# Two weight loads moved from SyncE's queue to ScalarE's at the start of a fused S5 scan and GeGLU kernel

## The chip, the cores and the metric

The kernel runs on one core of one Trainium2 chip. The metric is the device time of one execution in microseconds (us). Before the change three runs took 179.05 to 179.17 us, with a median of 179.15 us.

The engines are called PE (TensorE, matrix products), ACT (ScalarE), DVE (VectorE), POOL (GpSimd) and SP (SyncE, which here only issues DMAs). ACT can issue DMAs too, on a queue of its own.

## The reference

The input is x of 2048 tokens by 512 features. It is normalised, goes through a complex diagonal recurrence (S5) and, beside it, through a gated feed-forward block of width 1376, and the two are multiplied and added to x:

```python
def _B_ref(x, w_gate, w_up, w_down):
    return (_gelu(x @ w_gate) * (x @ w_up)) @ w_down

# _A_ref: Bu = x @ B_bar^T (complex, 512 states); h_t = Lam_bar * h_(t-1) + Bu_t
#         y = 2 * Re(h @ C^T) + x * Dskip
x = A_x
xn = _layernorm(x, axis=-1)
s = _A_ref(xn, A_Lambda_re, A_Lambda_im, A_B_re, A_B_im, A_C_re, A_C_im, A_log_dt, A_Dskip)
g = _silu(_B_ref(xn, B_w_gate, B_w_up, B_w_down))
return x + s * g
```

All arrays are in bfloat16. The weights `w_gate` and `w_up` are 512 by 1376 (1.4 MB each), `w_down` is 1376 by 512.

## The kernel before

**Stages.** The tokens are cut into four slabs of 512 (`NS = 4`), each of four tiles of 128 tokens (`M = 4`). The 512 features are four k slices of 128 (`KT = 4`). The 1376 columns of the gate and up weights are three pieces (`CH`): 0 to 512, 512 to 1024 and 1024 to 1376, the last one with 352 columns.

For every slab the kernel normalises x, turns it (a transposing DMA into `xnT`), multiplies it with the up and gate weights (`gate_tile`, one group of four matmuls for each piece), multiplies gate and up, turns the product (`at_t`), multiplies with `w_down` (`down_pair`), and beside this runs the recurrence (`half`: products with `BT`, then rotations and scans on DVE) and the output product with C (`y_tile`).

**The first slab is special.** Its up and gate products do not wait for the whole normalisation. For tile 0, ACT sums columns 320 to 512 (L411, the first activation that reads x) and DVE columns 0 to 320 (L414), DVE subtracts both partial means (L418, two halves), PE turns the centred tile with four small matmuls (`head_t`, L387; L400 for the tiles 1 to 3), and DVE and ACT copy the result into `W` (L391, L393, L402). For the tiles 1 to 3 ACT makes the whole mean (L423) and DVE subtracts it (L424). Then single matmuls (`up_rows`, L462, one for a tile, a k slice and a piece of 512 columns) and groups of four (`first_w`, L499, for the 352-column piece and for the gate weights) use the centred tile; the factor 1/std is put in when ACT takes the result out of PSUM (L471, L505). Seven dummy matmuls on a constant (L375) run on PE from the start.

**Loads.** The weights come in pieces, so that PE can begin early: `load_w("wu", k0, k1, c0, c1, end, landed)` loads the k slices k0 to k1 and the columns c0 to c1. The first up piece is k slice 0, columns 0 to 512 (128 KB); the 352-column up piece is all four k slices of the columns 1024 to 1376 (352 KB). All x and weight loads are issued by SP; ACT issues three loads of 1 KB each, the parameters of the recurrence (L333), before L411.

**Order.** Each operation is a step of a list (`Plan.add`). `ORDER` is a fixed list of step numbers that a planner wrote beforehand from a cost for each step (for a load: `end` and `landed` are the due times of its issue and its landing, in us) and that `Plan.run` follows: it gives the order of the instructions on every engine's queue. `SLOTS` fixes the buffer of each group: six PSUM banks for groups of 512 columns ("ps") and two for part groups ("pp"). A bank is used again when the engine that reads its result is through.

**Completion semaphores.** In the built program the DMAs of both queues take eight completion semaphores in turn, in the order in which the steps are emitted. A DMA that takes a semaphore for a second time has a wait in front of it, in the queue of the engine that issues it, until the DMA that held it before has landed. Before the change the first eight are the x tiles 0, 1 and 2 (SP), parameter 0 (ACT), an up piece (SP), parameter 1 (ACT), an up piece (SP) and parameter 2 (ACT); the DMAs from the ninth on are all SP's.

Of the kernel before, what the change touches and what calls it, by code (L numbers as in the profile page):

```python
# [17 lines left out]
PE, ACT, DVE, POOL, SP = "PE", "ACT", "DVE", "POOL", "SP"  # L18


ORDER = (
# [24 lines left out]
)  # L46
SLOTS = {
# [4 lines left out]
    ),  # L52
    "pp": (
        0, 1, 0, 1, 0, 1, 0, 1, 0, 0, 0, 1, 0, 1, 0, 1, 0, 1, 0, 1, 1, 0, 1, 0, 1, 1, 1, 0, 0, 0, 0, 1, 1, 0, 1, 0, 1, 0, 1,
    ),
    "U": (
        0, 1, 0, 2, 0, 1, 0, 2,
    ),
    "g2": (
        5, 0, 1, 4, 3, 0, 4, 2, 2, 0, 1, 5, 3, 1, 4, 5,  # L60
    ),
    "at": (
        2, 0, 1, 3, 2, 1, 0, 0, 0, 1, 2, 3, 2, 3, 0, 1,
    ),
    "gtA": (
        0, 0, 1, 1, 0, 1, 0, 1, 1, 0, 0, 0, 1, 1, 0, 0,
    ),
    "gtB": (
        1, 1, 0, 0, 0, 0, 1, 1, 1, 0, 0, 0, 0, 1, 0, 1,
    ),  # L70
    "ubA": (
        0, 1, 0, 0, 1, 1, 1, 0, 0, 0, 1, 1,
    ),
    "ubB": (
        0, 0, 1, 1, 1, 0, 0, 1, 0, 0, 1, 0,
    ),
    "yg": (
        0, 0, 1, 1, 0, 1, 0, 1, 0, 1, 1, 0, 0, 0, 1, 0, 1, 0,
    ),
    "ot": (  # L80
        1, 1, 1, 0, 1, 0, 0, 0, 0, 0, 0, 1, 1, 0, 1, 0, 1,
    ),
    "sk": (
        2, 3, 0, 1, 5, 7, 4, 6, 0, 1, 3, 2, 5, 4, 6, 7,
    ),
    "atT": (
        0, 1, 3, 0, 1, 1, 3, 2, 0, 3, 2, 1, 1, 2, 3, 0,
    ),
}

# [58 lines left out]
def kernel(  # L149
# [17 lines left out]
    nc = tc.nc  # L167
# [3 lines left out]
    F = 1376  # L171
    KT = D // P
# [9 lines left out]
    CH = [(0, 512), (512, 1024), (1024, F)]  # L182
# [6 lines left out]
    V, A, G, T = nc.vector, nc.scalar, nc.gpsimd, nc.tensor  # L189
# [6 lines left out]
    def sb(name, shape, dt=BF16):  # L196
        return consts.tile(shape, dt, name=name)
# [4 lines left out]
    wu = sb("wu", [P, KT, F])  # L202
# [10 lines left out]
    W2 = CH[1][1]  # L213
# [51 lines left out]
    def dma(eng, issue, land, emit, reads=(), writes=(), **kw):  # L265
        return pl.add(eng, issue, emit, reads, writes, lag=land, **kw)
# [11 lines left out]
    def dma_sp(end, landed, emit, writes, **kw):  # L278

        n = dma(SP, end - sp_at[0], landed - end, emit, writes=writes, after=list(sp_last), not_before=sp_at[0], svc=(1, 0.0, 0.0), **kw)  # L280
        sp_at[0] = end
        sp_last[:] = [n]

    def load_w(nm, k0, k1, c0, c1, end, landed):

        w, r = w_of[nm]
        dma_sp(end, landed, lambda: nc.sync.dma_start(out=w[:, k0:k1, c0:c1], in_=r[:, k0:k1, c0:c1]),  # L287
               [(nm, k, c) for k in range(k0, k1) for c in range(3) if c0 <= CH[c][0] < c1])

    def load_slab(s, **kw):  # L290
        dma(SP, 0.8, 4.0, lambda: nc.sync.dma_start(out=x_tok[:, s * M : (s + 1) * M, :], in_=x_r[:, s * M : (s + 1) * M, :]),
# [3 lines left out]
    def load_x(m, end, landed):  # L295
        dma_sp(end, landed, lambda: nc.sync.dma_start(out=x_tok[:, m, :], in_=x_r[:, m, :]), [("x", 0, m)])  # L296

    W1 = CH[0][1]
    load_x(0, 1.12, 2.92)
    load_x(1, 1.59, 3.35)  # L300
    load_x(2, 2.06, 3.75)
    load_w("wu", 0, 1, 0, W1, 2.53, 4.4)
    load_w("wu", 0, 1, W1, W2, 3.0, 4.95)
    load_w("wu", 1, 2, 0, W1, 3.47, 5.5)
    load_w("wu", 1, 2, W1, W2, 3.94, 6.05)
    load_x(3, 4.41, 6.6)
    load_w("wu", 2, 3, 0, W1, 4.88, 7.15)
    load_w("wu", 2, 3, W1, W2, 5.35, 7.7)
    load_w("wu", 3, 4, 0, W2, 5.82, 8.8)
    load_w("wu", 0, KT, W2, F, 6.29, 10.0)  # L310
    load_w("wg", 0, KT, W1, F, 6.76, 12.4)
    load_w("wg", 0, KT, 0, W1, 7.23, 14.0)
    for ri, src in enumerate((A_B_re, A_B_im)):
# [18 lines left out]
    for i, (t, v) in enumerate(((pv0[0:4, :], A_log_dt), (pv1[0:4, :], A_Lambda_im), (pv1[4:8, :], A_Lambda_re))):  # L332
        first = [dma(ACT, 0.48, 1.7, lambda t=t, v=v: A.dma_start(out=t, in_=v.rearrange("(k p) -> k p", p=P)),  # L333
                     writes=[("pv", i)], rank=900.0, not_before=0.8, after=first)]
# [440 lines left out]
    c1, s1 = cbt[:, :, 1], sbt[:, :, 1]  # L775
# [32 lines left out]
    for pt in range(NPT):  # L808
# [3 lines left out]
            out=C2[:, 0, pt, :], in0=CT[:, 0, pt, :], scalar=cre[:, pt : pt + 1], in1=tF[:, 1, :], op0=ALU.mult, op1=ALU.subtract),  # L812
            ["coef", ("CT", 0), ("tF",)], [("C2", 0, pt)], base=0.13)
        dve(512, lambda pt=pt: V.scalar_tensor_tensor(
            out=C2[:, 1, pt, :], in0=CT[:, 1, pt, :], scalar=ncre[:, pt : pt + 1], in1=tF[:, 0, :], op0=ALU.mult, op1=ALU.subtract),
# [104 lines left out]
```

## Time and profile before

| | |
|---|---|
| median of three runs | 179.15 us (179.05 to 179.17) |
| profiled execution, first to last instruction (span) | 176.9 us |
| PE busy | 172.1 us, 97% of the span |
| DVE busy | 154.6 us, 87% |
| ACT busy | 132.6 us, 75% |
| DMA queue used by SP | 18.52 MB, 46.7% of the 16 DMA engines' span |

The median is the time of the whole execution; the span leaves out what lies before the first and after the last instruction, 2.25 us here. Busy shares are averages over the span: an engine can be the limit in one stage and idle in another. Lines such as L411 are those of the kernel before; after the change the same lines stand three or four lines lower (L411 becomes L414, L462 becomes L465).

### The profile page before, as it was taken

How to read it: one execution, taken by the hardware profiler on the slowest of the kernel's cores; microseconds unless marked ns; L12 is line 12 of the kernel's file. 1: busy time of each engine (PE TensorE's matmuls, PEld its weight loads, DVE VectorE, ACT ScalarE, POOL GpSimd, SP SyncE). 2: the span in 40 equal slices, each digit the busy share in tenths (PEclk: the TensorE clock that was granted, in tenths of full speed). 3: DMA queues.
4: the chain of work that ended last, by engine and by line, in shares of the span. 5: the costliest groups of instructions: out<-in, count | busy, mean ns of one | idle time of the engine just before them, and what ended most of it. 6: DMA issues, size and time to landing. Idle time of an engine off the chain costs nothing.

```text
span 176.9 us, 2418 instructions
## 1 busy us (share of the span) xinstructions
PE 172.1 (97%) x834; PEld 82.3 (47%) x849; DVE 154.6 (87%) x253; ACT 132.6 (75%) x246; POOL 10.9 (6%) x25
## 2 busy tenths in 40 slices
PE   8999999999999999999999999999999999999992
PEld 2554544454454444444444444444444444444451
DVE  3743799999999988999999699999999999999343
ACT  6679999989999999956697665735898860793310
POOL 2640500000200000011000000000000000000000
PEclk9999999999999999999999999999999999999999
DMA  5999999997092730040057050063007300550531
GB/s 150 285 347 247 160 288 189 305 217 158 8 193 43 138 62 4 0 82 0 0 115 150 2 111 0 0 126 70 0 11 154 87 0 4 129 123 0 113 119 30
DMA packets 48467, 18.66 MB, mean 105 GB/s; under 512 B 40296, under 2 KB 48328, under 8 KB 48456
## 3 DMA queue, kind: packets, MB, share of 16 engines
q1 hardware_dynamic: 48432, 18.52, 46.7%
q8 instruction: 6, 0.10, 0.2%
q14 instruction: 5, 0.04, 0.1%
q10 hardware_dynamic: 24, 0.00, 0.0%
HBM read 6.46 MB, written 2.10 MB: 48 GB/s over the span
## 4 chain that ended last, share of the span: by engine, by line
PE 94%; DMA 2%; SPq 1%; issue 1%; DVE 0%
PE bank L536 31%; PE bank L564 21%; PE bank L615 16%; PE bank L579 16%; PE bank L499 7%; PE bank L462 3%; DMA wu<-in_B_w_up_dram 2%; SPq L296 1%; SPq L287 0%; DVE yg L585 0%; DVE ot L586 0%; PE bank L400 0%
## 5 line engine op out<-in xcount | busy, mean ns | idle before, releaser
L536 PEld LDWEIGHTS <-xnT 128*128 128x128 bf16 x288 | 28.1, 98 | 29.4
L564 PE MATMUL bank<-wd,atT 128*128 128x512 bf16 (+1 forms) x174 | 40.2, 379 | 0.1
L536 PE MATMUL bank<-wu,xnT 128*128 128x512 bf16 (+1 forms) x140 | 31.9, 356 | 0.1
L536 PE MATMUL bank<-wg,xnT 128*128 128x512 bf16 (+1 forms) x139 | 31.7, 356 | 0.3
L615 PE MATMUL bank<-xnT,BT 128*128 128x512 bf16 x128 | 30.9, 379 | 0.1
L646 DVE TENSOR_TENSOR_SCAN Fs<-rho,ini,W 128x512 bf16<-128x512 f32 x24 | 29.8, 1272 | 0.1
L579 PE MATMUL bank<-C,hst 128*128 128x512 bf16 (+1 forms) x134 | 29.7, 366 | 0.1
L564 PEld LDWEIGHTS <-atT 128*128 128x128 bf16 (+1 forms) x176 | 17.2, 98 | 20.3
L539 ACT ACTIVATE ubA<-bank 128x512 bf16<-128x512 f32 x24 | 14.6, 614 | 8.8 <-PE bank L536 8.3
L617 ACT ACTIVATE U<-bank 128x512 bf16<-128x512 f32 x32 | 19.1, 622 | 1.7 <-PE bank L615 1.7
L579 PEld LDWEIGHTS <-hst 128*128 128x128 bf16 x136 | 13.3, 98 | 14.0
L615 PEld LDWEIGHTS <-BT 128*128 128x128 bf16 x128 | 12.5, 98 | 14.3
L627 DVE TENSOR_TENSOR Q<-U,tab 128x4096 bf16<-128x4096 bf16 x8 | 18.3, 2287 | 0.7 <-ACT tab L715 0.6
L539 ACT ACTIVATE gtA<-bank 128x512 bf16<-128x512 f32 x24 | 14.8, 616 | 5.3 <-PE bank L536 4.6
L627 DVE TENSOR_TENSOR Q<-Fs,tab 128x4096 bf16<-128x4096 bf16 x8 | 18.3, 2285 | 0.1
L567 ACT ACTIVATE g<-bank 128x512 f32<-128x512 f32 x16 | 9.2, 594 | 12.1 <-PE bank L564 12.1
L585 DVE TENSOR_TENSOR yg<-bank,g 128x512 bf16<-128x512 f32 (+1 forms) x17 | 11.1, 655 | 5.0 <-PE bank L579 4.6
L539 ACT ACTIVATE ubB<-bank 128x352 bf16<-128x352 f32 x12 | 5.7, 475 | 6.6 <-PE bank L536 5.5
L838 ACT ACTIVATE junk<-x_tok 128x512 bf16<-128x512 bf16 x16 | 10.2, 649 | 0.0
L499 PE MATMUL bank<-wg,W 128*128 128x512 bf16 (+1 forms) x47 | 9.7, 356 | 0.1
L843 ACT ACTIVATE xna<-x_tok,nb,rs 128x512 bf16<-128x512 bf16 x12 | 9.6, 876 | 0.0
L575 ACT ACTIVATE bank<-sk 128x512 f32<-128x512 bf16 (+1 forms) x17 | 9.5, 577 | 0.1
(121 smaller groups left out, 190.0 us busy)
## 6 DMA issues: line engine op xcount, KB each, us to landing
out_dram<-ot SPq DMA_DIRECT2D x15, 128.0 KB, 1.8
x_tok<-in_A_x_dram SPq DMA_DIRECT2D x3, 512.0 KB, 5.6
wd<-in_B_w_down_dram SPq DMA_DIRECT2D x1, 1280.0 KB, 7.1
wg<-in_B_w_gate_dram SPq DMA_DIRECT2D x1, 864.0 KB
wu<-in_B_w_up_dram SPq DMA_DIRECT2D x6, 128.0 KB, 3.3
x_tok<-in_A_x_dram SPq DMA_DIRECT2D x4, 128.0 KB, 2.2
wg<-in_B_w_gate_dram SPq DMA_DIRECT2D x1, 512.0 KB, 7.8
wu<-in_B_w_up_dram SPq DMA_DIRECT2D x1, 352.0 KB, 3.9
```

The costliest lines, as they stand in the source:

```text
L499: T.matmul(ps[:, 0 : b - a], lhsT=xcT[:, k, m * P : (m + 1) * P], rhs=wt[:, k, a:b], start=(k == 0), stop=(k == KT - 1))
L536: T.matmul(ps[:, 0 : b - a], lhsT=xnT[:, s % 2, m, k, :], rhs=wt[:, k, a:b], start=(k == 0), stop=(k == KT - 1))
L539: acts(b - a, lambda: act(out=dst, in_=ps[:, 0 : b - a], func=AF.Copy if up else AF.Gelu_apprx_tanh), [key], [ok], table=None if up else " ...
L564: T.matmul(ps[:], lhsT=atT[:fs, k, iT * P : (iT + 1) * P], rhs=wd[:fs, k, :], start=(k == 0), stop=(k == NFT - 1))
L579: T.matmul(ps, lhsT=hst[s % 2][:, j // NPT, j % NPT, m * P : (m + 1) * P], rhs=C2[:, j // NPT, j % NPT, c0:c1], start=False, stop=(j == 2 ...
L585: dve(w, lambda: V.tensor_tensor(out=yg[iy][:, 0:w], in0=ps, in1=g2[ig][:, c0:c1], op=ALU.mult), [key, ("g2", gg)], [("yg", gy)])
L615: T.matmul(ps[:], lhsT=BT[:, ri, k, pt * P : (pt + 1) * P], rhs=xnT[:, s % 2, :, k, :], start=(k == 0), stop=(k == KT - 1))
L617: acts(512, lambda q=q, ri=ri, ps=ps: act(out=U[ui][:, ri, q, :], in_=ps[:], func=AF.Copy), [key], [("U", ug, q, ri)])
L627: dve(4096, lambda: V.tensor_tensor(out=Qf, in0=src.unsqueeze(1).to_broadcast(WQ), in1=table, op=ALU.mult), reads, ["Q"], rate=2.0)
L646: pl.add(DVE, 1.12 if s == 0 else 1.185, lambda ri=ri, q=q, pt=pt, first=first: V.tensor_tensor_scan(out=Fs[:, ri, q, :], data0=rho[:, pt ...
L838: acts(512, lambda i=i, fn=fn, sc=sc, m=m: act(out=junk()[:], in_=x_tok[:, s * M + m, :], func=fn, scale=sc, accum_out=sx[:, s, i, m : m + ...
L843: acts(512, lambda m=m: act(out=xn[m], in_=x_tok[:, s * M + m, :], func=AF.Identity, scale=rs[:, s, m : m + 1], bias=nb[:, s, m : m + 1]), ...
```

## The change

`load_w` gets a flag that puts a load on ACT's queue. Two loads use it: the first up piece, and the 352-column up piece. The other loads stay on SP, in the order of the listing without those two.

```diff
-    def load_w(nm, k0, k1, c0, c1, end, landed):
+    def load_w(nm, k0, k1, c0, c1, end, landed, act_queue=False):
         w, r = w_of[nm]
-        dma_sp(end, landed, lambda: nc.sync.dma_start(out=w[:, k0:k1, c0:c1], in_=r[:, k0:k1, c0:c1]),
-               [(nm, k, c) for k in range(k0, k1) for c in range(3) if c0 <= CH[c][0] < c1])
+        keys = [(nm, k, c) for k in range(k0, k1) for c in range(3) if c0 <= CH[c][0] < c1]
+        if act_queue:
+            dma(ACT, 0.43, landed - end, lambda: A.dma_start(out=w[:, k0:k1, c0:c1], in_=r[:, k0:k1, c0:c1]), writes=keys)
+            return
+        dma_sp(end, landed, lambda: nc.sync.dma_start(out=w[:, k0:k1, c0:c1], in_=r[:, k0:k1, c0:c1]), keys)
...
-    load_w("wu", 0, 1, 0, W1, 2.53, 4.4)
+    load_w("wu", 0, 1, 0, W1, 2.53, 4.4, act_queue=True)
...
-    load_w("wu", 0, KT, W2, F, 6.29, 10.0)
+    load_w("wu", 0, KT, W2, F, 6.29, 10.0, act_queue=True)
```

`ORDER` and `SLOTS` are written anew by the planner: the same 692 steps in another order and in other buffers, on every engine. On ACT the two loads follow the three parameter loads and stand ahead of the first activation on x. On PE the matmuls of the first slab change places: after the first tile's transposes come single up matmuls of the k slices 0 and 1, eight of them in a row before the first group on the 352-column piece, which before came after six. On SP the last x slab is loaded after the first transposing load of C and no longer before the transpose of slab 1, and the large part of `w_down` follows two transposes of `at` later.

More of the change, by code (lines that the diff above doesn't have):

```diff
@@ L48 @@
     "ps": (
[3 rows of a table removed]
[3 rows of a table added]
     ),
     "pp": (
-        0, 1, 0, 1, 0, 1, 0, 1, 0, 0, 0, 1, 0, 1, 0, 1, 0, 1, 0, 1, 1, 0, 1, 0, 1, 1, 1, 0, 0, 0, 0, 1, 1, 0, 1, 0, 1, 0, 1,
+        0, 0, 1, 0, 0, 1, 0, 1, 1, 1, 1, 0, 1, 1, 0, 0, 0, 0, 1, 1, 1, 1, 0, 0, 1, 0, 1, 0, 0, 1, 1, 0, 0, 0, 1, 1, 1, 0, 1,
     ),
     "U": (
-        0, 1, 0, 2, 0, 1, 0, 2,
+        1, 0, 2, 1, 0, 2, 0, 1,
     ),
     "g2": (
-        5, 0, 1, 4, 3, 0, 4, 2, 2, 0, 1, 5, 3, 1, 4, 5,
+        2, 1, 0, 5, 4, 2, 5, 3, 0, 5, 1, 3, 2, 1, 4, 0,
     ),
     "at": (
-        2, 0, 1, 3, 2, 1, 0, 0, 0, 1, 2, 3, 2, 3, 0, 1,
+        2, 1, 0, 3, 2, 0, 1, 0, 0, 2, 3, 1, 2, 0, 3, 1,
     ),
     "gtA": (
-        0, 0, 1, 1, 0, 1, 0, 1, 1, 0, 0, 0, 1, 1, 0, 0,
+        1, 1, 0, 1, 1, 1, 0, 0, 0, 1, 0, 1, 0, 1, 1, 0,
     ),
     "gtB": (
-        1, 1, 0, 0, 0, 0, 1, 1, 1, 0, 0, 0, 0, 1, 0, 1,
+        0, 0, 0, 1, 0, 1, 0, 0, 1, 1, 0, 1, 0, 0, 1, 1,
     ),
     "ubA": (
-        0, 1, 0, 0, 1, 1, 1, 0, 0, 0, 1, 1,
+        0, 0, 1, 1, 0, 1, 0, 1, 1, 0, 0, 1,
     ),
     "ubB": (
-        0, 0, 1, 1, 1, 0, 0, 1, 0, 0, 1, 0,
+        1, 1, 0, 1, 0, 1, 1, 0, 0, 1, 1, 0,
     ),
     "yg": (
-        0, 0, 1, 1, 0, 1, 0, 1, 0, 1, 1, 0, 0, 0, 1, 0, 1, 0,
+        0, 0, 1, 1, 1, 0, 1, 1, 1, 1, 0, 0, 0, 1, 0, 0, 1, 0,
     ),
     "ot": (
-        1, 1, 1, 0, 1, 0, 0, 0, 0, 0, 0, 1, 1, 0, 1, 0, 1,
+        1, 1, 1, 0, 0, 1, 1, 1, 0, 0, 0, 1, 1, 0, 1, 0, 1,
     ),
     "sk": (
-        2, 3, 0, 1, 5, 7, 4, 6, 0, 1, 3, 2, 5, 4, 6, 7,
+        2, 0, 1, 3, 5, 4, 6, 7, 2, 0, 3, 1, 7, 6, 4, 5,
     ),
     "atT": (
-        0, 1, 3, 0, 1, 1, 3, 2, 0, 3, 2, 1, 1, 2, 3, 0,
+        1, 3, 0, 0, 1, 2, 3, 2, 2, 0, 1, 3, 1, 2, 0, 0,
     ),
```

54 rows, old and new, of tables (ORDER, SLOTS) are left out of this document.

## Prediction

> **What bounds the kernel now.** I read the page first, then the chain that ended last in order of time, then the timeline of the first 24 us engine by engine. The page says who is busy, and what the chain of waits is made of:
>
> ```profile
> span 176.9 us, 2418 instructions
> PE 172.1 (97%) x834; PEld 82.3 (47%) x849; DVE 154.6 (87%) x253; ACT 132.6 (75%) x246; POOL 10.9 (6%) x25
> PE 94%; DMA 2%; SPq 1%; issue 1%; DVE 0%
> ```
>
> The chain in order of time shows where the other 6% lie (columns: start us, us, what):
>
> ```profile
> 1.18 0.41 SPq L296
> ...
> 2.58 0.43 SPq L287
> ...
> 3.06 3.89 DMA wu<-in_B_w_up_dram
> ...
> 6.99 1.35 PE bank L499 x8
> ...
> 8.78 0.60 PE bank L499 x4
> 9.38 0.86 PE bank L462 x4
> ...
> 172.01 1.76 PE bank L579 x16
> ```
>
> From 6.99 us, when the 352-column up piece has landed (issued at 3.06), to 173.77 us TensorE is the chain without a break. So the end is 6.99 us plus 166.8 us of matmuls that follow back to back, and only two things can move it: how much of TensorE's work is done by 7 us, and whether the new order leaves TensorE waiting later. An up matmul of 512 columns takes 0.86 / 4 = 0.215 us of the chain, a 352-column group of four 0.60 us. The span is 176.9 us, the median run 179.15 us; the 2.25 us between them I leave as they are, and every term below is added to the median.
>
> The first 7 us on ACT, on DVE and on TensorE (columns: start us, us, instruction):
>
> ```profile
> 1.66 0.32 ACTq L333 DMA_DIRECT2D pv<-in_A_Lambda_re_dram  x1
> ...
> 2.88 0.36 ACT L411 ACTIVATE junk<-x_tok 128x192 bf16<-128x192 bf16 x1 [0.67 <-DMA x_tok<-in_A_x_dram]
> 3.15 0.19 ACT L411 ACTIVATION_READ_ACCUMULATOR junk<-x_tok 128x1 f32 x1
> 3.44 0.63 ACT L423 ACTIVATE junk<-x_tok 128x512 bf16<-128x512 bf16 x1
> 3.97 0.19 ACT L423 ACTIVATION_READ_ACCUMULATOR junk<-x_tok 128x1 f32 x1
> 4.06 0.61 ACT L423 ACTIVATE junk<-x_tok 128x512 bf16<-128x512 bf16 x1
> ```
>
> ```profile
> 3.49 0.60 DVE L418 TENSOR_SCALAR xna<-x_tok,ma,mb 128x256 bf16<-128x256 bf16 x2
> 4.19 0.35 DVE L424 TENSOR_SCALAR xna<-x_tok,ma 128x512 bf16<-128x512 bf16 x1
> 4.46 0.28 DVE L391 COPY W<-bank 128x256 bf16<-128x256 bf16 x1
> 4.80 0.35 DVE L424 TENSOR_SCALAR xna<-x_tok,ma 128x512 bf16<-128x512 bf16 x1
> ```
>
> ```profile
> 3.90 0.66 PE L387 MATMUL bank<-ident,xna 128*128 128x128 bf16 x4
> 4.60 0.40 PE L400 MATMUL bank<-ident,xna 128*128 128x128 bf16 x4
> 4.84 0.38 PE L462 MATMUL bank<-wu,W 128*128 128x512 bf16 x1
> 5.21 0.40 PE L400 MATMUL bank<-ident,xna 128*128 128x128 bf16 x4
> ...
> 5.67 1.25 PE L462 MATMUL bank<-wu,W 128*128 128x512 bf16 x5
> ```
>
> The row to see is L411 on ACT: the partial mean of the first x tile. DVE's centring (L418) starts 0.61 us after it, TensorE's first transposes 1.02 us after it, the first up matmul 1.96 us after it. By 6.99 us TensorE has done three tiles' transposes and 1 + 5 = 6 up matmuls.
>
> **Part one: what ScalarE's queue now carries ahead of L411.** The two moved loads stand on ACT behind the three parameter loads and ahead of L411. In the built program a DMA takes one of eight completion semaphores in turn, over both queues, and one that takes a used semaphore waits until the earlier holder has landed. The first eight holders are x tile 0, 1, 2, parameter 0, an up piece, parameter 1, an up piece, parameter 2. The listing of the changed program then has, on ACT:
>
> ```
> L289 DMACopy wu<-in_B_w_up_dram 128x512    [waits DMAHW1]   holder before: x tile 1
> L289 DMACopy wu<-in_B_w_up_dram 128x4x352  [waits DMAHW3]   holder before: parameter 0
> L414 Activation junk,mb<-x_tok 128x192     [waits DMAHW0]   holder before: x tile 0  (L411 before the change)
> ```
>
> Before the change the ninth to twelfth DMAs were all SP's, where such a wait holds up only loads. Now the first of them stands in ACT's own order. The trace of before has no DMA waiting on ACT, so the price comes from x tile 1, the load issued at 1.18 us (the tile view of x_tok over 1.17 to 1.20 us holds it alone):
>
> ```profile
> DMA to landing us min/median/max: 2.2/2.2/2.2
> ```
>
> It lands at 3.38 us, which agrees with L423 starting at 3.44. ACT was free for a DMA at 1.66 + 0.32 = 1.98 us; it now waits until 3.4, issues two loads at the 0.43 us of the SP row plus 0.05 between issues, and starts the mean of tile 0 at about 3.4 + 0.48 + 0.48 = 4.36 us instead of 2.88: 1.48 us later. Bounds: an ACT issue took 0.32 us in the parameter row, which gives 4.15; a later x tile 1 would move it up one for one. [...]
>
> Then, by the same distances as before: L418 at 4.36 + 0.61 = 4.97, transposes at 5.38. Tile 1's mean no longer waits for its data: ACT reaches it 0.36 us behind the first one (0.27 to its accumulator read, and 0.09 as between 3.97 and 4.06), at 4.72, so DVE centres it when it is through with tile 0, at 5.53. The copy L391 follows at 5.80, the first up matmul at 5.80 + 0.38 = 6.18. Tile 2: mean at 5.34, centred 0.74 later at 6.08, transposable 0.41 later at 6.49. TensorE's new order is up, up, tile 2's transposes (0.22), up: 6.18 + 0.43 + 0.22 + 0.215 = 7.05 us, and tile 1's copies are done by then. So at 7.05 us it has three tiles' transposes and 3 up matmuls, where before had 6 at 6.99. **Lag: 3 x 0.215 + 0.06 = 0.70 us**; with 0.2 us either way for the issue time, 0.5 to 0.9.
>
> What the loads bring: SP's queue is two issues, 2 x 0.47 us, shorter. The first up piece, now issued at 3.4 instead of 2.11, lands by the 2.2 us of the x row at 5.6, by the 3.89 us of the wu row at 7.3, against 6.18 needed; with three pieces ahead of it instead of the 352-column one I take 5.8, no cost, and 0 to 1.1 as bounds. The 352-column piece, issued at 3.9 and by its own row landed at 7.8, is now asked for eight ups after 7.05, at 8.78: the wait that ended the chain's DMA part is gone, hidden by the up work that the new order puts ahead of it, and what is late instead is the x path. If the new order were empty of that work it would cost 7.8 - 7.05 = 0.75 us.
>
> **Part two: the order behind it.** The planner costed an ACT load at 0.43 us without the wait, so its whole order assumes TensorE about 1.4 us earlier than it will be. Where two engines meet with no slack, that shows as waits. I followed the bank releases up to 52 us. ACT's prices:
>
> ```profile
> 7.84 0.55 ACT L471 ACTIVATE at<-bank,rs 128x352 bf16<-128x352 f32 x1 [1.39 <-POOL ve L365]
> 8.29 0.62 ACT L423 ACTIVATE junk<-x_tok 128x512 bf16<-128x512 bf16 x1
> ...
> 11.41 0.36 ACT L688 ACTIVATE sbt<-ang 128x196 f32<-128x196 f32 x1
> ...
> 12.60 0.30 ACT L697 ACTIVATE sp<-sbt 128x128 bf16<-128x128 f32 x1
> ...
> 13.74 1.83 ACT L471 ACTIVATE at<-bank,rs 128x512 bf16<-128x512 f32 x3
> 15.59 1.28 ACT L505 ACT_TABLE_LOAD   x1
> ```
>
> A 512-column eviction takes (15.59 - 13.74) / 3 = 0.61 us from start to start, a 352-column one 0.45 (7.84 to 8.29), a sine 0.36, a spread 0.30. Tightest place: the gate group of tile 2 (columns from 1024) needs the bank of tile 3's first up group. From 7.05 us TensorE gets there after 28 ups, three 352-column groups, one tile's transposes and two gate groups of 0.86: 7.05 + 6.02 + 1.80 + 0.22 + 1.72 = 16.81 us. ACT cannot start the 352-column eviction of tile 1 before 11.53 (its last matmul starts at 11.13, and 7.84 is 0.40 behind the fourth matmul of the group at 6.99) and has six 512-column evictions, one more 352-column one, two sines and a spread up to that bank: 11.98 + 3.66 + 0.45 + 0.72 + 0.30 = 17.11. TensorE waits 0.3 us. The same count, through the gelu table load (1.28), gives ACT 21.9 against TensorE 21.75 at the bank of tile 0's last gate group: 0.15. Each count is good to some 0.3, so **0.45 us, bounds 0 to 1.0**. Beyond that the slab-1 transpose that TensorE needs at 31.7 is ready for SP at 26.9, which leaves the load 4.8 us (each us over that would cost one), and the banks from 32 to 52 us come free ahead of TensorE; I cost these at nothing, and the nearest miss is a rival below. The last twelve TensorE steps end with the same two half tiles, so the tail is unchanged: 0.
>
> **Sum:** 179.15 + 0.70 + 0.45 = 180.3 us.
>
> **Rivals.** (1) The clock stays low at the start. Two groups of matmuls of the first 24 us by form (last columns: busy us, mean ns):
>
> ```profile
> L462 PE MATMUL bank<-wu,W 128*128 128x512 bf16 x31 | 8.0, 379 | 0.1
> ...
> L375 PE MATMUL bank<-const-bfloat16-1.0 128*128 128x512 bf16 x7 | 3.1, 627 | 0.8 <-PEq L904 0.8
> ```
>
> The seven dummies are slow (627 against 379 ns for the same shape; 3.1 / 7 = 0.45 us each), tile 0's transposes still took 0.66 us, tile 1's 0.40. So the switch comes at about 4.5 us, and the change puts 1.48 us of nothing between 3.9 and 5.38. If it then came as much later as dummies and transposes lasted here (3.4 us, so 7.9), the four matmuls that fit between 6.18 and then would cost 0.45 instead of 0.215 each: 0.9 us, 181.2 us. The dummies alone fill most of that stretch, so I give it 0.12. [...]
>
> (2) ACT waits for the last x slab. The new SP order loads it behind a transposing load of C, no longer ahead of the slab-1 transpose, and ACT's first step on it (at 36.3 us by the count above) stands ahead of two evictions, 1.1 us of them, that TensorE needs at 38.0. The nearest rows, two transposing loads and a slab (third row's landing: the tile view over 21.84 to 21.90 us):
>
> ```profile
> 19.38 2.42 SPq L314 DMA_TRANSPOSE BT<-in_A_B_im_dram  x1
> 21.85 0.58 SPq L291 DMA_DIRECT2D x_tok<-in_A_x_dram  x1
> ...
> 29.57 6.21 SPq L807 DMA_TRANSPOSE hst<-in_A_C_im_dram  x1
> ```
>
> ```profile
> DMA to landing us min/median/max: 5.1/5.1/5.1
> ```
>
> The slab-1 transpose leaves at 26.9 and holds SP some 2 us; with 2.42 us for C the slab is issued at 31.4 and lands at 36.5, in time; with 6.21 us it lands at 40.3, ACT is 4.0 us late and TensorE 3.4. The 6.21 us stood behind the 1280 KB of wd, which the new order puts after C, so 2.42 is nearer. Halfway, TensorE loses some 1.5 us: 181.8 us, chance 0.12.
>
> (3) The other side, faster: ACT's loads go out at once. If nothing held them, the loads would take 1.98 to 2.94 us, L411 would start 0.06 us late and TensorE could work nearly without a break from about 5.7 us: nine ups by 7.05 instead of six, 0.65 us won, less 0.1 of bank waits: 178.6 us. The decisive point is whether x tile 1 lands by 2.0 us. Its row says 3.38, with L423 at 3.44 beside it, so 0.06.
>
> (4) No change: lag at its lower bound 0.5 us, no bank waits, and 0.2 us back from shorter SP issues: 179.4 us, 0.06.
>
> **How the numbers follow.** A measurement of this kernel can tell about 0.2%, 0.36 us, from no change (three runs within 0.12 us). The forecast, slower by 1.15 us, has the chance 0.64, rivals 0.12, 0.12, 0.06, 0.06. Its own bounds are 0.5 to 0.9 plus 0 to 1.0, 179.65 to 181.05. The range reaches from 179.5 to 182.0: it takes in the late clock and half of the slab rival, and leaves out 0.06 faster, most of 0.06 no change and 0.06 of the worst slab case. Faster by over 0.36 us: 0.06; within it: 0.07 (rival 4 and a sliver of the forecast); slower: 0.87.
>
> **What would show it.** In the profile after: an idle ACT until about 3.4 us, its two DMA issues at 3.4 and 3.9, the first-tile mean at 4.36 (2.88 before), first transposes at 5.4, first up matmul at 6.2, and no DMA in the chain after that; then ACT named as releaser for TensorE waits of 0.1 to 0.4 us near 17 and 22 us. Tile 0's and 1's transposes at 0.66 us each would be rival 1; an ACT step on x_tok waiting for DMA near 36 us rival 2. I am wrong in the main step if the first-tile mean starts at 3.0, and wrong in the sum if it starts at 4.4 and the span is not longer by 0.5 us or more, since from 7 us on TensorE has nothing to give back.

## The result, and the profile after

The changed kernel is slower. The comparison gives a ratio of 1.0119 to the kernel before, 95% interval 1.0071 to 1.0167, which is 181.2 us at the 179.1 us measured beside it. That ratio leaves out runs over 1.5% above the fastest of their kernel; here the wide spread is the changed kernel's own, as the experiments show, so all runs count below. The four runs took 180.36, 181.96, 183.39 and 183.55 us (median 182.68); with seven more, taken later, they lie between 179.95 and 183.55 us around 182.3 us. The kernel before stays within 178.35 and 179.4 us in all but one of its runs. The profiled execution is the 183.55 us one.

The page of after: span, busy times, and the shares of the chain that ended last.

```profile
span 181.8 us, 2414 instructions
PE 174.7 (96%) x833; PEld 83.2 (46%) x849; DVE 154.4 (85%) x253; ACT 129.4 (71%) x244; POOL 11.3 (6%) x25
PE 82%; ACT 11%; DMA 3%; issue 1%; DVE 1%; SPq 0%
```

Its chain in order of time, to 20 us (start us, us, what):

```profile
1.18 2.30 DMA x_tok<-in_A_x_dram
...
3.50 3.91 DMA wu<-in_B_w_up_dram
...
7.45 1.01 PE bank L465 x2
8.46 0.43 PE bank L403 x4
8.89 3.66 PE bank L465 x9
12.54 0.60 PE bank L502 x4
...
15.08 0.88 ACT at L474 x2
...
18.61 1.17 ACT at L474 x2
```

Three things are new beside the chain of before, which was TensorE from 6.99 us on. It now begins with x tile 1 and then with an up piece that ScalarE issues at 3.50 and that lands at 7.41. Nine up matmuls take 3.66 us, 0.41 us each, where before four took 0.86. And from 15 us ScalarE is in it (11% of the span; before it was not named).

ScalarE, VectorE and TensorE of after (start us, us, instruction, and in brackets the idle time before it and what ended it):

```profile
3.50 0.85 ACTq L289 DMA_DIRECT2D wu<-in_B_w_up_dram  x2
4.40 0.36 ACT L414 ACTIVATE junk<-x_tok 128x192 bf16<-128x192 bf16 x1 [2.19 <-DMA x_tok<-in_A_x_dram]
4.76 0.61 ACT L426 ACTIVATE junk<-x_tok 128x512 bf16<-128x512 bf16 x1
```

```profile
4.89 0.60 DVE L421 TENSOR_SCALAR xna<-x_tok,ma,mb 128x256 bf16<-128x256 bf16 x2 [1.58 <-ACT junk L414]
```

```profile
5.29 0.65 PE L390 MATMUL bank<-ident,xna 128*128 128x128 bf16 x4 [1.39 <-DVE xna L421]
...
6.01 0.60 PE L403 MATMUL bank<-ident,xna 128*128 128x128 bf16 x4
7.45 1.01 PE L465 MATMUL bank<-wu,W 128*128 128x512 bf16 x2 [0.83 <-DMA wu<-in_B_w_up_dram]
8.26 0.63 PE L403 MATMUL bank<-ident,xna 128*128 128x128 bf16 x4
8.68 3.86 PE L465 MATMUL bank<-wu,W 128*128 128x512 bf16 x9
12.38 0.76 PE L502 MATMUL bank<-wu,W 128*128 128x352 bf16 x4
```

The reader is to see the row 3.50 of ScalarE, then the two holes of TensorE: one from the dummies' end at 3.9 to 5.29, ended by the late first tile, and one to 7.45, ended by the late first up piece.

Where the time went I count so: for each profile, the matmul columns that TensorE has still to start at a time t, at 0.2155 us for 512 (sixteen in a row take 3.45 us in the chain of before, at 144.46), less those of before. Most profiles lack 15 or 16 of TensorE's matmul records; these are counted in, where a step of 0.43 us at full clock (twice the usual one) shows that a record is missing. This **lag** of after is 1.7 us at 7 us, 2.7 at 9, 4.4 at 14, 4.8 at 60, and TensorE ends 4.84 us later (178.60 against 173.76). So nine tenths of the loss is made before 14 us.

### The profile page after: what moved, and what is told of

Its sections match the earlier page's. It is cut to its first block, busy times and chain, and to the rows that moved or that the text cites. A ratio compares the mean times of both kernels' runs of the same rounds, so it can differ in the third digit from the quotient of the medians.

```text
span 181.8 us, 2414 instructions
## 1 busy us (share of the span) xinstructions
PE 174.7 (96%) x833; PEld 83.2 (46%) x849; DVE 154.4 (85%) x253; ACT 129.4 (71%) x244; POOL 11.3 (6%) x25
## 4 chain that ended last, share of the span: by engine, by line
PE 82%; ACT 11%; DMA 3%; issue 1%; DVE 1%; SPq 0%
PE bank L539 29%; PE bank L567 21%; PE bank L582 15%; PE bank L618 12%; PE bank L465 3%; ACT at L474 3%; ACT gtA L508 2%; DMA wu<-in_B_w_up_dram 2%; ACT U L620 2%; ACT xna L846 1%; DMA x_tok<-in_A_x_dram 1%; ACT junk L841 1%; ACT gtB L508 1%; ACT L508 1%; PE bank L502 1%
## 5 line engine op out<-in xcount | busy, mean ns | idle before, releaser
L567 PE MATMUL bank<-wd,atT 128*128 128x512 bf16 (+1 forms) x171 | 39.4, 379 | 0.3
L588 DVE TENSOR_TENSOR yg<-bank,g 128x512 bf16<-128x512 f32 (+1 forms) x17 | 11.1, 652 | 5.6 <-PE bank L582 4.7
L465 PE MATMUL bank<-wu,W 128*128 128x512 bf16 x31 | 10.3, 461 | 0.9 <-DMA wu<-in_B_w_up_dram 0.8
L474 ACT ACTIVATE at<-bank,rs 128x512 bf16<-128x512 f32 (+1 forms) x12 | 7.3, 661 | 5.0 <-POOL rs L369 4.5
L841 ACT ACTIVATE junk<-x_tok 128x512 bf16<-128x512 bf16 x16 | 10.7, 708 | 0.0
L502 PE MATMUL bank<-wg,W 128*128 128x512 bf16 (+1 forms) x47 | 10.2, 356 | 0.1
```

Source lines behind the costliest of these rows:

```text
L465: T.matmul(ps[:], lhsT=xcT[:, k, m * P : (m + 1) * P], rhs=wu[:, k, a:b], start=(k == 0), stop=(k == KT - 1))
L474: acts(b - a, lambda: act(out=at[i][:, a:b], in_=ps[:, 0 : b - a], func=AF.Copy, scale=rs[:, 0, m : m + 1]), [key, ("rs", 0, m)], [("at", ...
L502: T.matmul(ps[:, 0 : b - a], lhsT=xcT[:, k, m * P : (m + 1) * P], rhs=wt[:, k, a:b], start=(k == 0), stop=(k == KT - 1))
L567: T.matmul(ps[:], lhsT=atT[:fs, k, iT * P : (iT + 1) * P], rhs=wd[:fs, k, :], start=(k == 0), stop=(k == NFT - 1))
L841: acts(512, lambda i=i, fn=fn, sc=sc, m=m: act(out=junk()[:], in_=x_tok[:, s * M + m, :], func=fn, scale=sc, accum_out=sx[:, s, i, m : m + ...
```

## The experiments

My theory from these rows: ScalarE's wait costs what the prediction said, but the two holes that follow make TensorE's clock slow, for a time that differs from run to run; the rest is the new order, in which ScalarE gives banks back late. Rivals: the new order alone, the second queue as such, or the wait alone.

**The changed kernel again, twice** (no edit).

> The changed kernel once more, for its spread. My theory: TensorE's hole from 3.9 to 5.3 us and the second one to 7.4 us leave its matmuls slow (0.43 us for 512 columns) for a time that differs from run to run, so the runs spread over 180.3 to 183.6 us again, and the profile shows the switch to 0.215 us somewhere between 5 and 13 us; time and switch go together, 0.21 us for each slow up matmul. Rival, a cause after 13 us (ScalarE's bank waits, the loads): the first 13 us are alike in all profiles and the spread comes later.

> The changed kernel once more, one look, for a profile with another place of the clock's stretches. Theory: stretches of 3.41 us, and the time goes with how many of the up matmuls before 13 us take 0.43 instead of 0.215 us: 180.0 to 180.6 with none or few, 183.0 to 183.6 with ten or more. Rival: the time differs by over 1 us from another run of this kernel at the same number of slow matmuls.

Measured: 179.95 to 183.33 us (median 182.13), and 182.30 us in the separate run. The windows of that run (us, busy time of each engine with its count, then granted clock, DMA share, GB/s) and its TensorE:

```profile
4.00:8.00 4.00, 2.14 (x18) 1.29 (x19) 2.21 (x10) 3.36 (x11) 1.71 (x3) 0.96 0.92 259
8.00:11.00 3.00, 3.00 (x8) 1.06 (x7) 2.82 (x12) 0.72 (x2) 1.45 (x5) 0.50 1.04 376
11.00:12.00 1.00, 1.00 (x7) 0.52 (x6) 0.00 (x0) 0.00 (x0) 0.53 (x1) 0.95 1.05 374
```

```profile
6.88 0.59 PE L465 MATMUL bank<-wu,W 128*128 128x512 bf16 x2 [0.71 <-DMA wu<-in_B_w_up_dram]
...
7.53 3.79 PE L465 MATMUL bank<-wu,W 128*128 128x512 bf16 x9
```

Here the clock is first high, two ups take 0.59 us together, and then the granted clock falls to 0.50 from 7.7 to 11.1 us, for 3.4 us, and nine ups take 3.79. What the slow up matmuls lost over their pace at full clock is 2.13 us in the first profile, 1.23 in the second (183.21 us) and 1.69 in the third (182.30 us); the first up piece landed at 7.41, 7.98 and 6.83. So the time does not go with the slow matmuls alone, as I had it: the landing of the first up piece moves it too. Together they account for it: the start of the first up plus this loss (9.58, 9.25 and 8.57 us) falls in step with the lag at 14 us (4.42, 4.00 and 3.12), and the times less that lag are 179.1, 179.2 and 179.2. No profile caught one of the fast runs near 180.

**Twelve dummies.**

```diff
-    dummies(7)
+    dummies(12)
```

> Twelve dummy matmuls instead of seven, so that TensorE is busy to about 5.2 us; nothing else changes. If the slow matmuls come from the hole after the dummies: ups take 0.215 us from 7.45 us on, the time is 180.4 to 181.4 us (0.45 late start of the first up aside from the forecast's terms: first up at 7.45 still waits for its weights), and the runs lie within 0.6 us of each other. Rival, the dummies do not matter: 180.4 to 183.6 us as before, with slow ups to about 12 us. Rival, the second hole (6.6 to 7.45 us) alone is enough: slow ups come back after it, 182 to 183.5 us.

Measured: 180.67 us, 180.18 to 180.97, ratio 1.0098 (1.0079 to 1.0116).

```profile
0.76 4.80 PE L378 MATMUL bank<-const-bfloat16-1.0 128*128 128x512 bf16 x12 [0.76 <-PEq L907]
...
6.08 0.59 PE L465 MATMUL bank<-wu,W 128*128 128x512 bf16 x2
...
6.74 2.11 PE L465 MATMUL bank<-wu,W 128*128 128x512 bf16 x9
9.80 0.76 PE L502 MATMUL bank<-wu,W 128*128 128x352 bf16 x4 [0.95 <-DMA wu<-in_B_w_up_dram]
```

```profile
3.78 5.98 DMA wu<-in_B_w_up_dram
```

Only the hole before the first transposes is filled, ScalarE still issues at 3.37, and every up takes 0.215 us. The spread goes from 3.4 to 0.8 us and the median falls by 1.5. So the slow clock behind that hole is the main cause of both. Three parts of the expectation missed: the spread is 0.8 and not 0.6 us, the first piece landed early in this profile (5.92), and the 352-column piece, issued at 3.78, landed at 9.76 and held TensorE for 0.95 us. No load was changed here, and why the piece came early is open; a first piece up to 0.95 us later would have been hidden in that last wait. In the changed kernel the slow ups hide the wait.

**The same hole in the kernel before**, to see whether the hole alone makes ups slow.

```diff
-    dummies(7)
+    dummies(3)
```

> The kernel before with three dummy matmuls instead of seven: TensorE idles from 2.2 to 3.9 us and nothing else changes. [...] Rival (a hole of 1.7 us does nothing; ScalarE's and SyncE's loads alone make the spread of the changed kernel): 178.6 to 179.3 us.

Measured: 180.04 us, 179.37 to 180.97, ratio 1.0063 (1.0040 to 1.0085).

```profile
3.81 0.65 PE L387 MATMUL bank<-ident,xna 128*128 128x128 bf16 x4 [1.61 <-DVE xna L418]
...
6.01 2.19 PE L462 MATMUL bank<-wu,W 128*128 128x512 bf16 x5
```

Loads, order and the first mean (2.79) are as before, the idle time is where nothing could run anyway, and still five ups take 2.19 us instead of 1.25; the lag is 1.0 at 8 us and stays between 0.9 and 1.2. The rival (178.6 to 179.3 us) fails: here a hole of 1.61 us cost some 1 us by itself.

**Parameters from GpSimd's queue**, so that ScalarE's loads wait for nothing.

```diff
-lambda t=t, v=v: A.dma_start(out=t, ...
+lambda t=t, v=v, i=i: (G if i else A).dma_start(out=t, ...
```

> Parameters 1 and 2 are loaded from GpSimd's queue, so that ScalarE's two loads are among the first eight holders of completion semaphores and wait for nothing. Theory (the wait for x tile 1 in ScalarE's queue is the cause): ScalarE issues at 1.4 and 1.9 us, the first-tile mean starts at 2.9 to 3.0, transposes at 3.9 to 4.0, first up before 5.5, no slow ups after that; 178.4 to 179.3 us. Rival (the new order costs by itself): 179.5 us or more although the mean starts at 2.9. Rival (a load from ScalarE's queue is slow whenever it is issued, 3.9 us): first piece lands at 5.3, first up at 5.4 to 5.5, 179.2 to 179.8 us.

Measured: 184.06 us, ratio 1.0268 (1.0242 to 1.0293).

```profile
1.37 0.85 ACTq L289 DMA_DIRECT2D wu<-in_B_w_up_dram  x2
...
2.97 0.36 ACT L414 ACTIVATE junk<-x_tok 128x192 bf16<-128x192 bf16 x1 [0.76 <-DMA x_tok<-in_A_x_dram]
```

```profile
7.07 0.16 PE L676 MATMUL bank<-ident,pv 8*128 8x8 bf16 x1 [2.31 <-DMA pv<-in_A_Lambda_re_dram]
```

The expected time failed, though the mean starts at 2.97: parameter 2, issued from GpSimd at 2.61, landed at 6.94, and TensorE's order has its transpose ahead of the ups. A hole of 2.3 us took the place of the old ones, nine ups ran slowly behind it, and it tells nothing about the price of the wait. It does answer one rival: from ScalarE's queue the first piece took 2.65 us (1.37 to 4.02), so that queue is not slow as such.

**Both loads back on SyncE's queue, new order.** In the first kernel the 352-column piece (step 11) stands behind the second up piece, in the other one last.

```diff
-27, 3, 11, 0, 1, 2, 4, 6, 5, 7, 8, 9, 10, 12,
+27, 0, 1, 2, 3, 4, 11, 6, 5, 7, 8, 9, 10, 12,    # 352 third
+27, 0, 1, 2, 3, 4, 6, 5, 7, 8, 9, 10, 11, 12,    # 352 last
```

> Both loads back on SyncE's queue at the places that they had before (the first up piece behind x tile 2, the 352-column piece behind the second up piece), everything else in the new order. Theory: the new order costs only the bank waits, 0 to 0.5 us: 179.0 to 179.7 us, first-tile mean at 2.9, first up at 4.9. Rival (the order is the cause): 180.5 us or more.

> Both loads back on SyncE's queue in the new order, the 352-column piece behind all other up pieces (the other run had it third). Theory (the new order of TensorE's work asks for eleven up matmuls ahead of the 352-column groups, and the DMA engines are full from 2 us on, so some piece is late wherever the loads stand): first up at 4.9, the 352-column piece issued at 5.9 lands at 9.5 to 10 and is asked for at 7.3 to 8: a wait of 1.5 to 2.5 us; 180.0 to 182.5 us. Rival (the new order is good if the loads follow it, ScalarE's queue is the whole loss): 178.9 to 179.5 us.

Measured: 180.70 us (180.21 to 182.90), ratio 1.0089 (1.0070 to 1.0108), and 182.88 us (181.16 to 185.31), ratio 1.0145 (1.0119 to 1.0172).

```profile
8.12 3.79 PE L465 MATMUL bank<-wu,W 128*128 128x512 bf16 x9 [2.02 <-DMA wu<-in_B_w_up_dram]
```

```profile
11.81 0.76 PE L502 MATMUL bank<-wu,W 128*128 128x352 bf16 x4 [3.51 <-DMA wu<-in_B_w_up_dram]
```

In both the first mean is at 2.9 and the first up at 4.9 to 5.1, and both wait for weights: the first 2.02 us for the second piece of k slice 1, behind the 352-column piece, the second 3.51 us for the 352-column piece (more than I expected). By the numbers the rival holds in the first; in the second the rival (178.9 to 179.5 us) fails and the theory's range is passed as well. In both the loads' places do not suit the new order, so these runs do not weigh the order by itself.

**Only the 352-column piece on ScalarE's queue.**

```diff
-    load_w("wu", 0, 1, 0, W1, 2.53, 4.4, act_queue=True)
+    load_w("wu", 0, 1, 0, W1, 2.53, 4.4)
-27, 3, 11, 0, 1, 2, 4, 6, 5,
+27, 11, 0, 1, 2, 3, 4, 6, 5,
```

> Only the 352-column piece on ScalarE's queue; the first up piece back on SyncE's, behind x tile 2. ScalarE still waits for x tile 1 ahead of the first mean. Theory: issue at 3.4, mean at 3.9 (0.48 earlier than with two loads), transposes at 4.9, first up piece landed at 4.4 to 5, first up at 5.7; hole in TensorE of 1.0 us instead of 1.4: runs between 179.5 and 182.5 us, median about 0.5 us under that of the changed kernel. Rival (the first up piece on ScalarE's queue is not part of the loss): the same median as the changed kernel within 0.3 us.

Measured: 181.01 us (180.63 to 181.44), ratio 1.0113 (1.0092 to 1.0134).

```profile
4.73 0.65 PE L390 MATMUL bank<-ident,xna 128*128 128x128 bf16 x4 [0.82 <-DVE xna L421]
...
7.24 2.75 PE L465 MATMUL bank<-wu,W 128*128 128x512 bf16 x9
```

The mean starts at 3.83, the first up at 5.85, the second hole is gone, and the median is 1.1 us under that of the changed kernel (0.5 expected). Here also, behind a hole of 0.82 us, ups are slow until 8.55 us.

**The wait taken out**, first as it is, then with TensorE's hole filled.

```diff
-lambda t=t, v=v: A.dma_start(out=t, ...
+lambda t=t, v=v, i=i: (nc.sync if i == 2 else A).dma_start(out=t, ...
-24, 25, 26, 27, 3, 11, 0, 1, 2, 4, 6, 5,
+24, 25, 26, 3, 0, 1, 2, 4, 27, 6, 5,
...
-29, 30, 44, 46,
+29, 30, 44, 11, 46,
# the second kernel besides: parameter transposes and what follows (38, 39, 40) behind two more ups
-34, 36, 38, 65, 50, 37, 51, 35, 39, 47, 17, 67, 68, 69, 66, 21, 70, 40,
+34, 36, 65, 50, 37, 51, 35, 47, 17, 67, 68, 69, 66, 21, 70, 77, 71, 38, 39, 40,
```

> The wait is taken out of ScalarE's queue: parameter 2 goes out from SyncE's queue behind the second up piece, so that the first up piece on ScalarE's queue is the eighth DMA and gets a free completion semaphore (issued at 1.7 us), and the 352-column piece stands on ScalarE behind the means of tiles 0 and 1. Theory: first-tile mean at 2.9, transposes at 3.95, first up at 4.8 to 5.0 us, so the 0.70 us lag and the first late landing are gone; left are the wait for the 352-column piece (issued at 4.0 to 4.4, landing at 8 to 9.8, asked for at about 7.2: 1 to 2.5 us, with a slow stretch of clock behind it in some runs) and 0.6 us of the new order: 179.7 to 182 us, the fastest runs under 180.0. Rival (without the wait the change is neutral or better): 178.6 to 179.2 us.

> As the run without the wait, and the two parameter transposes on TensorE (with their copy on VectorE and the step on GpSimd that follows) moved behind the first four up matmuls, so that TensorE has no hole between 4 and 6 us. [...] Rival (the loss in that run was the new loads' places and not the slow clock): 181.4 to 182.0 us as there.

Measured: 181.71 us (181.37 to 181.96), ratio 1.0150 (1.0129 to 1.0171); and 180.29 us (180.04 to 180.75), ratio 1.0072 (1.0049 to 1.0095).

TensorE of the second:

```profile
3.90 0.65 PE L390 MATMUL bank<-ident,xna 128*128 128x128 bf16 x4
4.45 0.61 PE L403 MATMUL bank<-ident,xna 128*128 128x128 bf16 x4
4.86 1.06 PE L465 MATMUL bank<-wu,W 128*128 128x512 bf16 x2
...
8.52 0.76 PE L502 MATMUL bank<-wu,W 128*128 128x352 bf16 x4
```

In both the first mean starts at 2.9: the wait was in ScalarE's queue and nowhere else. The first one misses 180.0 because parameter 2 landed late and made a hole of 0.92 us, after which ups were slow to 9.5 us. With that step moved behind four ups, TensorE has no hole, the lag at 9 us is 0.4, and 1.4 us come back. The wait for the 352-column piece that I expected did not come; its group starts at 8.52 unhindered. What is left, 1.0 us at 14 us and 1.35 at 60, lies mostly behind the first ups.

**ScalarE relieved**: the twelve-dummies kernel with gelu replaced by a plain copy.

```diff
-func=AF.Gelu_apprx_tanh
+func=AF.Copy
```

> The run with twelve dummies, with gelu replaced by a plain copy everywhere (the output is not the reference's): ScalarE has no table load of 1.28 us near 18 us and each gate eviction is about 0.1 us shorter. Theory (from 14 to 60 us TensorE loses 0.5 to 0.6 us because ScalarE gives banks back late in the new order): that loss shrinks to 0.2 us or less and the time falls from 180.67 to 180.1 to 180.4 us. Rival (the loss is not ScalarE's): 180.5 to 180.9 us.

Measured: 180.30 us (179.59 to 181.35), ratio 1.0083 (1.0055 to 1.0111). The time is spread too widely to decide: the theory's range and the rival's both lie within it. The profiles, one of each kernel, speak for the theory. The shares of the chain with gelu and without:

```profile
PE 80%; ACT 12%; DMA 5%; issue 1%; DVE 0%; SPq 0%; ACTq 0%
```

```profile
PE 93%; DMA 4%; issue 1%; DVE 0%; SPq 0%; ACTq 0%
```

ScalarE leaves the chain. With gelu TensorE's matmuls wait for a bank twice between 14 and 60 us, 0.19 us at 22.4 us and 0.25 at 34.5, both times until ScalarE has evicted a gate group (`gtB`); here is ScalarE's part of that kernel's chain:

```profile
18.36 1.28 ACT L508
...
22.14 0.45 ACT gtB L508
...
34.36 0.36 ACT gtB L542
...
34.77 2.27 PE bank L539 x11
```

Without gelu no matmul starts late there by more than 0.035 us, and none in the old order with the hole.

**A version that might beat both**: the old order, and only the 352-column piece on ScalarE's queue, put in the list behind two means.

```diff
-    load_w("wu", 0, KT, W2, F, 6.29, 10.0)
+    load_w("wu", 0, KT, W2, F, 6.29, 10.0, act_queue=True)
-30, 31, 11, 44, 32,
+30, 31, 44, 11, 32,
```

> The old order throughout; of the change only the 352-column up piece on ScalarE's queue, behind the means of tiles 0 and 1, so that its wait for a completion semaphore (x tile 2) stands ahead of a step that needs x tile 2 anyway. A version that could beat both kernels: SyncE's queue is one issue (0.47 us) shorter and the x path keeps its start at 2.9 us. Theory: the piece is issued at 3.9 to 4.1 us instead of 3.06 and lands at 7.5 to 8.5 us, asked for at 7.0: TensorE waits 0.5 to 1.5 us, and since the DMA engines are full from 2 us on nothing is won elsewhere: 179.2 to 180.5 us. Rival (a second queue brings the loads in sooner): 178.2 to 178.8 us. Rival (the new order was the whole loss): 178.8 to 179.2 us.

Measured: 179.86 us (179.37 to 180.26), ratio 1.0056 (1.0038 to 1.0074).

```profile
7.99 1.35 PE L502 MATMUL bank<-wu,W 128*128 128x352 bf16 x8 [0.99 <-DMA wu<-in_B_w_up_dram]
```

The first mean stayed at 2.79. Issued at 3.31 instead of 3.06 (3.9 to 4.1 expected) the piece landed at 7.95 instead of 6.95, and TensorE waited for it as expected. No version here beats the kernel before.

## Why the prediction was right, and where it was not

**The wait in ScalarE's queue: right, step by step.** Issue predicted at 3.4, first mean at 4.36, centring 4.97, transposes 5.38; measured 3.50, 4.40, 4.89, 5.29. Four profiles have the issue at 3.36 to 3.63, each with x tile 1's landing (3.34 to 3.61) just ahead; with the wait out, the mean is back at 2.9.

**The lag of 0.70 us: the mechanism was right, the term that failed is the landing of the first up piece** ("I take 5.8, no cost, and 0 to 1.1 as bounds"). It landed at 7.41, 7.98 and 6.83 in the changed kernel, and early only in the two kernels with twelve dummies (5.92 and 6.21); the first up came at 7.45, 8.02, 6.88, 6.08 and 6.25 against 6.18 predicted. I had leaned towards the 2.2 us of a row issued when the DMA engines were hardly busy (share 0.29 from 1 to 2 us); the 3.89 us of the row issued among full ones (0.90) was nearer, and 4.35 us lies past it. In the two where the piece came early, the lag at 8 us was 0.6, within the 0.5 to 0.9 forecast.

**The 352-column piece: wrong where it shows.** "The wait that ended the chain's DMA part is gone" held only behind slow ups. At full clock, with twelve dummies, it was asked for behind two and then nine ups in a row (not eight, as the section on the change says) at 8.85 us (8.78 predicted) and landed at 9.76 instead of 7.8.

**Rival 1, the clock, took place on top of the forecast.** I gave it 0.12 and 0.9 us; slow up matmuls cost 1.23, 1.69 and 2.13 us in the three profiles, and beside the late first piece it is the large term of the loss (twelve dummies gave 1.5 us back). The step that failed is "The dummies alone fill most of that stretch", on which the chance of 0.12 rested: behind the hole of 1.39 us (and 0.83 us more) nine ups of the first profile took 0.41 us each, and behind holes of 1.25 and 0.71 us the third had two ups at the usual pace (0.59 us) and then nine at 0.40 (3.63 us of its chain). Its price was also short by its own rows: dummies (3.1 us) and tile 0's transposes up to the switch (0.6) lasted 3.7 us, and no run shows the 3.4 us that I took for them.

**Part two, 0.45 us of bank waits: the mechanism and the sum were right, the places only in part, and that is luck.** From 14 to 60 us TensorE waits for ScalarE twice in each of the three profiles of the changed kernel and with twelve dummies, 0.42 to 0.44 us together; with ScalarE relieved it does not wait. The first wait (0.18 to 0.19 us, behind the gelu table load, at 22.4 us with twelve dummies and 25.0 in the 183.55 us run) fits the one forecast with 0.15 near 22. The 0.3 us forecast near 17 us are not there: no matmul starts late between 14 and 22 us. In their place stands a wait of 0.24 to 0.25 us at 34.5 and 37.1 us, in the stretch from 32 to 52 us that I had costed at nothing. Behind 60 us, costed at nothing, the lag moves by less than 0.1 us to the end in all four.

**The other rivals.** ScalarE never waited for the last slab: its list of waits has x_tok only at the start.

```profile
ACT junk L414 <- DMA x_tok<-in_A_x_dram: 2.2, 1, 2.2
...
ACT junk L426 <- DMA x_tok<-in_A_x_dram: 0.3, 1, 0.3
```

The loads did not go out at once (3.50), and a lag at its lower bound was not seen.

**The sum.** 180.3 us is near what the kernel takes in its fastest runs (179.95 to 180.75) and with the clock held up (180.67, there by other terms than mine: 0.6 for the x path, 1.0 for the 352-column piece, 0.4 for the banks); the ratio's 181.2 us lies above it, and eight of the eleven runs lie above 181.5, because two terms add up that I had as alternatives: the late x path of the forecast and the slow clock of rival 1. The direction held. The range, 179.5 to 182.0, holds for the ratio's 181.2 us, and only because it reached for the clock rival; six of the eleven runs and their median lie above it, so that it held is in part luck.

## What to carry to other kernels

A DMA put on a computing engine's queue brings its waits with it, the one for a reused completion semaphore too (here the first mean went from 2.88 to 4.40 us, and back to 2.9 without the wait): count the DMAs in order of emission and look at who held the ninth's semaphore, before asking what the load itself costs. Price a hole in TensorE's first microseconds not by its length but by what runs slowly behind it (five ups took 2.19 instead of 1.25 us behind one where nothing could run anyway), and take a sudden spread of times as a sign to look for one (here 3.4 us, and 0.8 with the hole before the first transposes filled). In the kernel before, the DMA share is already 0.78 to 1.05 in every microsecond from 2 to 12, and no version with loads on a second queue was faster; the piece that left 0.25 us later landed 1 us later.

## What the runs showed of the hardware

All numbers here are read from the profiles of this case. Behind the dummies and before 13 us TensorE's timelines name these holes (idle time of 0.2 us and more, in brackets the start of the row that ended it), with these paces behind them. At the usual pace two ups take 0.59 us from the start of the first to the end of the last, four 1.03, five 1.25 and nine 2.10.

| run | hole, us | behind it |
|---|---|---|
| kernel before | none | transposes 0.66 us at 3.90, 0.40 at 4.60; five ups 1.25 at 5.67 |
| without the wait, filled | none | two ups 1.06 at 4.86, two 0.59 at 6.34 |
| only 352 | 0.82 (4.73) | two ups 1.17 at 5.85, nine 2.75 at 7.24 |
| without the wait | 0.92 (5.60) | two ups 1.06 at 6.09, nine 3.17 at 7.37 |
| after | 1.39 (5.29), 0.83 (7.45) | two ups 1.01 at 7.45, nine 3.86 at 8.68 |
| after, second profile | 1.52 (5.42), 1.59 (8.02) | transposes 0.40 at 6.04; two ups 1.01 at 8.02, nine 2.97 at 9.25 |
| after, third profile | 1.25 (5.15), 0.71 (6.88) | two ups 0.59 at 6.88, nine 3.79 at 7.53 |
| kernel before, three dummies | 1.61 (3.81) | five ups 2.19 at 6.01, two 0.59 at 9.23 |
| parameters from GpSimd | 2.31 (7.07) | two ups 0.59 at 7.40, nine 3.79 at 8.06 |
| 352 third on SyncE | 2.02 (8.12) | nine ups 3.79 at 8.12 |
| 352 last on SyncE | 3.51 (11.81) | four ups 1.48 at 12.40 |
| twelve dummies | 0.95 (9.80) | four ups 1.03 at 10.39 |
| twelve dummies, no gelu | 0.26 (5.15) | two ups 0.59 at 6.25, nine 2.10 at 6.91 |
| old order, 352 on ScalarE | 0.20 (5.28), 0.99 (7.99) | five ups 1.25 at 5.74, two 0.59 at 9.18 |

So the length of a hole does not tell the pace behind it: there were slow ups behind 0.82 and 0.92 us and none behind 0.95 and 0.99 (before the first two no matmul had run at the usual pace, before the last two the ups had). What decides it, these runs do not show.

Four profiles show both ends of a low granted clock. By the means of the windows in which it changes, it is 0.50 from 7.56 to 10.98 us and from 7.7 to 11.1 (second and third profile of after), from 8.18 to 11.58 (parameters from GpSimd) and from 8.18 to 11.60 (352 third on SyncE), about 3.4 us each time. The windows of the 183.55 us run show 1.00 all the way from 0 to 15 us, though the nine ups took 3.66 us of the chain there: the pace of the matmuls is the safer witness.

The same load, issued at 3.35 to 3.63 us from the same queue, took 2.55, 2.86, 3.48, 3.91 and 4.35 us to land in five profiles. What sets that is not settled.
